# Attention with two head mixings and a feed-forward block: second batch in float32, sums in two steps, weights' conversion spread to step 90

## The chip, the cores and the metric

One core of one Trainium2 chip. The core has TensorE (PE; its weight loads are shown apart as PEld), VectorE (DVE), ScalarE (ACT), GpSimd (POOL) and SyncE (SP), which issues the DMAs; the engines run side by side, each in its own program order, and wait for each other by semaphores. The metric is the device time of one execution in microseconds; before the change it is 1026.39 us, the median of three runs (1025.78 to 1027.22).

## The reference

Four batches of 448 tokens, twelve heads of 64. The scores of all heads of a token pair are mixed by a 12 x 12 matrix before the softmax, and the attention weights by another one after it. The result, 1792 x 768, goes through a feed-forward block with 2048 hidden units. Weights come as float64.

```python
scores = scale * np.matmul(q, k.transpose(0, 1, 3, 2))
scores = np.einsum('bhij,hg->bgij', scores, w_pre)
scores = scores - np.max(scores, axis=-1, keepdims=True)
attn = np.exp(scores)
attn = attn / (np.sum(attn, axis=-1, keepdims=True) + 1e-09)
attn = np.einsum('bhij,hg->bgij', attn, w_post)
out = np.matmul(attn, v)                      # then x = out, heads side by side
h = x @ w_in
g = h * (1.0 / (1.0 + np.exp(-1.702 * h)))
return (g @ w_out).astype(np.float32)
```

## The kernel before

The work is written as a Python loop over steps, and what a step issues is the program's order on every engine; no scheduler moves it afterwards. A step i handles ten query rows of all twelve heads (120 partitions, 448 columns); 45 steps make a batch, 180 the attention. In the order of its data a group of ten rows goes through:

- scores (`scores`, lines 223 to 247): per pair of heads and chunk of 120 rows a product of q and k into two PSUM banks, copied by ScalarE and sent to a DRAM buffer `sd`, from which `gather` (line 264) reads ten rows of all heads, four steps ahead;
- `mix` (line 279): a float32 product with the 120 x 120 mixing matrix, issued one step ahead;
- `peak` (line 286), the negated row maximum on VectorE; `expo` (line 293), the exponential on ScalarE, which also sums the row; line 299, GpSimd's small epsilon-and-scale of that sum; `inverse` (line 304), VectorE's reciprocal of it;
- in batch 0 `weigh_mix` (line 309): GpSimd scales the 120 x 120 post-mixing matrix `wp` by the reciprocals, and `post_whole` (line 319) multiplies e by it in float32, four products a step, two steps behind; `keep_whole` copies the result to p;
- in batches 1 to 3 GpSimd weighs e (line 329), ScalarE writes its upper half in fp16 (line 337), GpSimd the rest (line 343), and `post` (lines 356 to 358) runs twelve fp16 products, three steps behind; ScalarE writes the upper half of p (line 379), VectorE subtracts the lower one (line 383);
- `context`: six head pairs per chunk of 120 rows, p times v: line 397 in float32 for batch 0 (8 products a pair), line 408 in fp16 halves for the others (24 products a pair), for which v is read twice, once for its size and once to be split.

Beside it run *jobs*: pieces of side work with a first step, an engine, a cost and what they come after. `run_jobs` issues in each step what is due, as long as an engine's tokens last; each step refills the tokens. `convert` makes one slice of w_in or w_out (16 in all) out of float64: three fetches, per piece five integer operations on VectorE (lines 484 to 504), a sum of squares on ScalarE, then for the slice the sum over partitions (`join_w`, by `add_all`, lines 104 to 109: a product with ones on TensorE and, right behind it in the order, VectorE's reduction of that product), its scale, an upper half on ScalarE (line 532), a lower half on VectorE (line 537) and a store to DRAM (`wd`). The slices begin at steps 5n - 6. The feed-forward work is cut into quanta of six fp16 products (lines 588 and 627), put between the attention's steps at 2.15 a step once the first batch's x is there (step 58), and dense after step 192. It fetches the converted slices from `wd` (`fetch_w`).

Of the kernel before, what the change touches and what calls it, by code (L numbers as in the profile page):

```python
# [18 lines left out]

B, H, S, D = 4, 12, 448, 64  # L20
DM, DFF = 768, 2048
NT = B * S
GI = 10
# [8 lines left out]
NS = 8  # L32
# [6 lines left out]
def attention_then_feed_forward(ctx, tc, q, k, v, w_pre, w_post, w_in, w_out, out):  # L39
# [29 lines left out]
    w_mix = keep.tile([KG, GI, H], F32, name="w_mix")  # L69
    wp = flow.tile([KG, H, GI], F32, name="wp", tag="th", bufs=2)  # L70
    wp1 = keep.tile([KG, H, GI], F16, name="wp1")
# [31 lines left out]

    def add_all(m, parts):

        p, n = parts.shape
        t = last_pp[-1][:, 512 - 16:512 - 16 + n]
        nc.tensor.matmul(t, ones[:p, :], parts, start=True, stop=True)
        nc.vector.tensor_reduce(m, t, axis=AX.X, op=ALU.add)


# [29 lines left out]

    def join(name, b):
        add_all(top_of(name, b), st["m" + name, b])

    def scale(name, b):

        m = top_of(name, b)
        e = stat.tile([128, 1], F32, name=f"e{name}_{b}", tag="e" + name)
        s = stat.tile([128, 1], F32, name=f"s_{name}{b}", tag="s" + name)
        root_bits(e, m)  # L150
        nc.vector.reciprocal(s, e)
        nc.vector.tensor_scalar_mul(s, s, 2.0 ** -50)
        nc.vector.tensor_scalar_mul(e, e, 2.0 ** 63)
        st["e" + name, b], st["s" + name, b] = e, s
        if name == "v":
            nc.vector.tensor_scalar(
                ex[:, b:b + 1], e, e_wp, 2.0 ** -12, op0=ALU.mult, op1=ALU.mult
            )
            if b == 0:
                xs = st["xs"] = keep.tile([128, 1], F32, name="xs")  # L160
                nc.vector.reciprocal(xs, ex[:, 0:1])

# [60 lines left out]
    def scores(b, c, pr, tag=("gen", 3)):  # L223

        i0, n = chunk(b, c)
        two = [bank(f"qk_{b}_{c}_{pr}_{x}", *tag) for x in range(2)]
        done = open_banks[-2:] if tag[0] == "gen" else []
        w = NPAIR // THIRDS
        if b < 2:
            qf, kf = st["q", b, pr // w], st["k", b, pr // w]  # L230
            for x in range(2):
                rs = slice(x * D, (x + 1) * D)
                nc.tensor.matmul(  # L233
                    two[x][:n, :S], qf[rs, pr % w, i0:i0 + n], kf[rs, pr % w, :],
                    start=True, stop=True,
                )
            return two, done
        qp, kp = st["qp", b, pr // w], st["kp", b, pr // w]
        terms = ((0, 0), (0, 1), (1, 0))
        for t, (i, j) in enumerate(terms):  # L240
            for x in range(2):
                rs = slice(x * D, (x + 1) * D)
                nc.tensor.matmul(  # L243
                    two[x][:n, :S], qp[rs, i, pr % w, i0:i0 + n], kp[rs, j, pr % w, :],
                    start=t == 0, stop=t == len(terms) - 1,
                )
        return two, done
# [41 lines left out]
    def expo(i):  # L289
        K = rows_of(steps[i][1])[1] * H  # L290
        e = flow.tile([KG, S], F32, name=f"e_{i}", tag="e", bufs=3)
        sm = stat.tile([KG, 1], F32, name=f"sm_{i}", tag="sm")
        nc.scalar.activation(  # L293
            e[:K], row.pop(("mx", i))[:K, :S], AF.Exp, bias=row.pop(("nm", i))[:K, 0:1],
            scale=1.0, accum_out=sm[:K, 0:1],
        )
        rs = stat.tile([KG, 1], F32, name=f"rs_{i}", tag="rs")
        by = 2.0 ** -10 if steps[i][0] else 1.0
        nc.gpsimd.tensor_scalar(rs[:K], sm[:K], 1e-9, by, op0=ALU.add, op1=ALU.mult)  # L299
        row["e", i], row["rs", i] = e, rs  # L300

# [60 lines left out]
    def mixed_to(i):  # L362
        b, g = steps[i]
        n = rows_of(g)[1]
        c, off = g // GPC, (g % GPC) * GI
        if off == 0:
            shape, kind = ([CP, NR, H, CI], F32) if b == 0 else ([CP, 2, NR, H, CI], F16)
            st["p", b, c] = mixed.tile(shape, kind, name=f"p_{b}_{c}", tag="p")
        p = st["p", b, c]
        if b == 0:  # L370
            return p.rearrange("p r h i -> p (r h) i")[:, :, off:off + n]
        return p.rearrange("p t r h i -> p t (r h) i")[:, :, :, off:off + n]
# [13 lines left out]
    def context(b, c, pr):  # L386
# [5 lines left out]
        w = H // THIRDS  # L392
        if b == 0:
            for jc in range(NR):
                for d in range(2):
                    h = 2 * pr + d
                    nc.tensor.matmul(
                        av[d * D:(d + 1) * D, pr % 3, :],
                        st["v", 0, h // w][:, h % w, jc * D:(jc + 1) * D],
                        st["p", 0, c][:, jc, h, :n],  # L400
                        start=(jc == 0), stop=(jc == NR - 1),
                    )
            return av
# [18 lines left out]
    def x_upper(b, c, half, av):  # L422
        i0, n = chunk(b, c)
        by = st["xs"] if b == 0 else 2.0 ** -15
        nc.scalar.activation(x_of(b)[:, 0, 3 * half:3 * half + 3, i0:i0 + n], av, AF.Copy, scale=by)

    def x_lower(b, c, half, av):
        i0, n = chunk(b, c)
        x = x_of(b)[:, :, 3 * half:3 * half + 3, i0:i0 + n]
        by = st["xs"] if b == 0 else 2.0 ** -15  # L430
        nc.vector.scalar_tensor_tensor(
# [3 lines left out]
    def x_size(b, c, half):  # L435
        i0, n = chunk(b, c)
        square_sum(x_of(b)[:, 0, 3 * half:3 * half + 3, i0:i0 + n],
                   st["mx", b][:, 2 * c + half:2 * c + half + 1], "A")

    def join_x(b):  # L440
        e = gs[:, b, 0:1]
        add_all(e, st["mx", b])

# [20 lines left out]
    def convert(kind, s, first):  # L464
# [45 lines left out]

        def join_w():
            t["n"] = stat.tile([128, 1], F32, name=f"{nm}_n", tag="wn")
            add_all(t["n"], t["m"])

# [31 lines left out]
        for a in range(NP):  # L546
# [11 lines left out]
            sizes.append(job(first, "A", 0.7, lambda a=a: size(a), after=[(last, 1)]))  # L558
        j = job(first, "D", 0.2, join_w, after=[(x, 1) for x in sizes])
        j = job(first, "D", 0.9, scale_w, after=[(j, 0)])  # L560
# [172 lines left out]
    for b in range(1, B):  # L733
        z = GPB * b
        sizes = {}
        if b == 1:
            for i in range(THIRDS):
                for name in "kq":
                    job(z - 23 + 4 * i, None, 0, lambda name=name, i=i: load_whole(name, 1, i), urgent=True)
        for name, first, ready in (("k", z - 25, z - 17), ("q", z - 23, z - 17), ("v", z - 8, z + LAG + 7)):  # L740
            if b == 1 and name != "v":
                continue
            sq = []
            for i in range(THIRDS):
# [3 lines left out]
                a["stage"][1].append(sq[-1])  # L748
            jn = job(0, "D", 0.2, lambda name=name, b=b: join(name, b), after=[(x, 1) for x in sq], urgent=True)
            sizes[name] = job(0, "D", 0.7, lambda name=name, b=b: scale(name, b), after=[jn], urgent=True)  # L750
            for i in range(THIRDS):
# [4 lines left out]
                a["stage"][1].extend([up, lo])  # L756
        if b > 1:
            job(0, "D", 0.4, lambda b=b: mixing(b), after=[sizes["k"], sizes["q"]], urgent=True)

    conv_done = {}  # L760
    for s in range(NS):
        for kind in range(2):
            n = s * 2 + kind
            conv_done[kind, s] = convert(kind, s, n * 5 - NPAIR if n > 1 else EARLY + 10 * n)

# [132 lines left out]
    sq = [job(1 + 2 * i, {"A": 1.6}, 0, lambda eng, i=i: squares("v", 0, i, eng, 2), urgent=True) for i in range(THIRDS)]  # L898
    j = job(1, "D", 0.2, lambda: join("v", 0), after=sq, urgent=True)
    job(1, "D", 0.9, lambda: scale("v", 0), after=[j], urgent=True)  # L900


# [49 lines left out]
    while quanta or i < N + LAG + 12:  # L952
# [8 lines left out]
        if i + 1 < N:  # L961
            mix(i + 1)
        if 0 <= i - 2 < GPB:
            post_whole(i - 2)
        if 0 <= i - 3 < GPB:
            keep_whole(i - 3)
            spend("A", 0.57)
        if GPB <= i - LAG - 1 < N:
            keep_upper(i - LAG - 1)
            spend("A", 0.55)  # L970
        if 0 <= i - 1 < GPB:
            weigh_mix(i - 1)
# [8 lines left out]
        if i < N:  # L981
            peak(i)
            spend("D", 0.62)
            expo(i)
            spend("A", 0.82)
        run_jobs(i)
# [3 lines left out]
        if owed >= 1 and do_quantum(i):  # L990
            owed -= 1
            slot()
        if GPB <= i - LAG < N:
            post(i - LAG)
# [5 lines left out]
        for b, c, pr in at_context.pop(i, []):  # L1000
# [7 lines left out]
            if c == NCH - 1 and pr == NPAIR - 1:  # L1008
                z = i
                a = job(z + 2, "D", 0.2, lambda b=b: join_x(b), urgent=True)  # L1010

                def finish(b=b, z=z):
                    scale_x(b)
                    x_done[b] = cur[0] + 1
                job(z + 3, "D", 0.9, finish, after=[a], urgent=True)
        slot()
        while owed >= 1 and do_quantum(i):
            owed -= 1
            slot()
        if GPB <= i - LAG - 1 < N:  # L1020
            keep_lower(i - LAG - 1)
            spend("D", 0.64)
        if i < N:
            inverse(i)
            spend("D", 0.15)
        owed = min(owed, 3.0)
# [44 lines left out]
```

## Time and profile before

| | |
|---|---|
| median of three runs | 1026.39 us |
| profiled execution | 1027.42 us, span 1025.7 us |
| PE / DVE / ACT / POOL busy | 925.0 / 628.8 / 605.2 / 354.5 us |
| mean granted TensorE clock | 0.961 |
| DMA | 198.19 MB, mean 193 GB/s |
| chain that ended last | PE 62%, DVE 17%, ACT 8%, DMA 8%, issue 3% |

Busy times are unions within an engine; products on TensorE overlap, so the time from one start to the next tells what a product costs, not its own length. The steps can be told by the row maxima of line 286, one a step: step 0 starts at 34.8 us, step 45 at 196.6, step 58 at 257.9, step 90 at 444.2, step 103 at 497.8, step 179 at 864.1.

### The profile page before, as it was taken

The numbers are of one execution on the slowest core, as the hardware profiler recorded it, in microseconds if no ns is written. First come the engines' busy times: TensorE is split into PE (matmuls) and PEld (weight loads), VectorE is DVE, ScalarE is ACT, GpSimd is POOL, SyncE is SP. The second block draws the span as 40 slices with busy tenths as digits, with TensorE's granted clock in tenths as the row PEclk, the third lists the DMA queues.
The fourth block names the chain that finished last, engine by engine and source line by source line (L and its number), as shares of the span: only waits on it lengthen the run. The fifth ranks groups of instructions, "written<-read, shape, count | busy, mean of one in ns | idle before, by whom it ended". The sixth has DMA issues, their size and how long they took to land.

```text
span 1025.7 us, 19868 instructions
## 1 busy us (share of the span) xinstructions
PE 925.0 (90%) x7344; PEld 542.4 (53%) x7344; DVE 628.8 (61%) x1389; ACT 605.2 (59%) x1380; POOL 354.5 (35%) x536
## 2 busy tenths in 40 slices
PE   5678878877899889999899999999899999999998
PEld 4345555544455444555455555656455666555554
DVE  5658786698976796554644575555645565443334
ACT  3666768677577676765657657656656564323332
POOL 0111111145433455343533454334534444001221
PEclk9888999888999998999999999999999999999999
DMA  8988979768557656654676647546654341234322
GB/s 301 289 275 313 332 267 323 259 197 245 190 198 244 232 187 181 192 172 131 202 225 207 202 150 234 166 130 179 212 164 146 108 148 64 93 123 151 118 93 85
DMA packets 66565, 198.19 MB, mean 193 GB/s; under 512 B 7668, under 2 KB 32372, under 8 KB 66468
## 3 DMA queue, kind: packets, MB, share of 16 engines
q1 hardware_dynamic: 66064, 196.83, 59.4%
q8 instruction: 58, 0.95, 0.4%
q14 instruction: 39, 0.32, 0.1%
q10 hardware_dynamic: 404, 0.09, 0.1%
HBM read 140.27 MB, written 56.62 MB: 192 GB/s over the span
## 4 chain that ended last, share of the span: by engine, by line
PE 62%; DVE 17%; ACT 8%; DMA 8%; issue 3%; POOL 1%; SPq 0%; ACTq 0%; DVEq 0%; POOLq 0%
PE po L627 19%; PE h L588 18%; PE mx L279 8%; PE av L408 4%; PE qk L243 3%; PE pp L356 2%; PE pp L358 2%; PE pp L357 2%; DVE w_p L537 2%; DMA sd<-sc 2%; ACT waste L96 2%; DVE w_f L504 2%; DMA w<-in_moe_w_out_dram 2%; DVE nm L286 2%; ACT e L293 1%
## 5 line engine op out<-in xcount | busy, mean ns | idle before, releaser
L627 PE MATMUL po<-g,wt 128*128 128x448 f16 x1152 | 243.8, 355 | 11.3 <-DVE th L609 6.8
L588 PE MATMUL h<-x,wt 128*128 128x448 f16 x1152 | 244.1, 356 | 3.9 <-ACT sc L253 2.9
L279 PE MATMUL mx<-r,wa 120*120 120x448 f32 x360 | 183.3, 592 | 40.0 <-ACT e L293 29.7
L343 POOL TENSOR_TENSOR a<-w,a 120x448 f16<-120x448 f32 x135 | 150.8, 1117 | 130.2 <-issue 71.5
L627 PEld LDWEIGHTS <-wt 128*128 128x128 f16 x1152 | 109.4, 99 | 130.0 <-issue 45.1
L588 PEld LDWEIGHTS <-wt 128*128 128x128 f16 x1152 | 109.2, 98 | 117.0 <-issue 31.2
L329 POOL TENSOR_SCALAR w<-e,rs 120x448 f32<-120x448 f32 x135 | 88.2, 653 | 227.3 <-DVE rs L304 217.8
L337 ACT ACTIVATE a<-e,rs 120x448 f16<-120x448 f32 x135 | 91.0, 674 | 106.1 <-DVE rs L304 106.1
L657 DVE SCALAR_TENSOR_TENSOR acc<-po,ct,acc 128x448 f32<-128x448 f32 x141 | 96.1, 682 | 74.3 <-PE po L627 72.2
L293 ACT ACTIVATE e<-mx,nm 120x448 f32<-120x448 f32 x180 | 113.6, 631 | 31.2 <-POOL wr L309 25.4
L609 DVE SCALAR_TENSOR_TENSOR th<-th,h 128x448 f32<-128x448 f32 x64 | 39.7, 620 | 137.8 <-ACT th L606 137.8
L606 ACT ACTIVATE th<-h,ct 128x448 f32<-128x448 f32 x64 | 40.5, 633 | 140.2 <-PE h L588 129.6
L253 ACT COPY sc<-qk 120x448 f32<-120x448 f32 (+1 forms) x186 | 89.6, 532 | 41.8 <-PE qk L233 28.9
L286 DVE TENSOR_REDUCE nm<-mx 120x1 f32<-120x448 f32 x180 | 108.9, 605 | 1.9 <-PE mx L279 1.9
L356 PE MATMUL pp<-wp,a 120*112 120x120 f16 x540 | 95.7, 220 | 14.8 <-DVE p L383 14.3
L279 PEld LDWEIGHTS mx<-r,wa 120*120 120x120 f32 x360 | 61.6, 193 | 83.9 <-ACT e L293 47.0
L299 POOL TENSOR_SCALAR rs<-sm 120x1 f32<-120x1 f32 x180 | 56.8, 315 | 115.8 <-ACT e L293 103.8
L358 PE MATMUL pp<-wp,a 120*112 120x120 f16 x540 | 95.1, 219 | 0.0
L357 PE MATMUL pp<-wp,a 120*112 120x120 f16 x540 | 94.9, 218 | 0.0
L383 DVE TENSOR_TENSOR p<-pp,p 112x480 f16<-112x480 f32 x135 | 87.2, 647 | 5.9 <-ACT p L379 5.9
L356 PEld LDWEIGHTS <-a 120*112 120x112 f16 x540 | 71.5, 132 | 26.9 <-DVE p L383 12.1
L357 PEld LDWEIGHTS <-a 120*112 120x112 f16 x540 | 71.8, 133 | 15.9 <-issue 9.5
(126 smaller groups left out, 1258.1 us busy)
## 6 DMA issues: line engine op xcount, KB each, us to landing
wt<-wd SPq DMA_DIRECT2D x64, 768.0 KB
r<-sd SPq DMA_DIRECT2D x176, 210.0 KB
sd<-sc SPq DMA_DIRECT2D x72, 420.0 KB
w<-in_moe_w_in_dram SPq DMA_DIRECT2D x24, 512.0 KB
w<-in_moe_w_out_dram SPq DMA_DIRECT2D x24, 512.0 KB
wd<-w_p SPq DMA_DIRECT2D x16, 768.0 KB
sd<-sc SPq DMA_DIRECT2D x24, 308.0 KB
out_dram<-acc SPq DMA_DIRECT2D x24, 224.0 KB
```

The lines of the kernel that those rows point to most:

```text
L253: (nc.scalar.copy if engs[x] == "A" else nc.vector.tensor_copy)(t[:n, x, :], two[x][:n, :S])
L279: nc.tensor.matmul(mx[:K, :S], st["wa", b][:K, :K], row.pop(("r", i))[:K, :], start=True, stop=True)
L286: nc.vector.tensor_reduce(nm[:K], row["mx", i][:K, :S], axis=AX.X, op=ALU.max, negate=True)
L293: nc.scalar.activation(e[:K], row.pop(("mx", i))[:K, :S], AF.Exp, bias=row.pop(("nm", i))[:K, 0:1], scale=1.0, accum_out=sm[:K, 0:1],)
L337: nc.scalar.activation(a1[:K], row.pop(("e", i))[:K], AF.Copy, scale=row.pop(("rs", i))[:K, 0:1])
L343: nc.gpsimd.tensor_tensor(a2[:K], row.pop(("w", i))[:K], row["a1", i][:K], op=ALU.subtract)
L356: nc.tensor.matmul(o, a1[:K, js], wp1[:K, :, :n], start=True, stop=False)
L357: nc.tensor.matmul(o, a1[:K, js], wp2[:K, :, :n], start=False, stop=False)
L358: nc.tensor.matmul(o, a2[:K, js], wp1[:K, :, :n], start=False, stop=True)
L588: nc.tensor.matmul(h, w[:, i, c, fc * 128:(fc + 1) * 128], x[:, j, c, :], start=(n == 0), stop=(n == len(terms) - 1),)
L627: nc.tensor.matmul(po, w[:, j, fc, e * 128:(e + 1) * 128], g[:, i, fc, :], start=(n == 0), stop=(n == len(terms) - 1),)
L657: nc.vector.scalar_tensor_tensor(a, po, c, a, op0=ALU.mult, op1=ALU.add)
```

## The change

A constant WHOLE = 2 takes the place of the tests for batch 0: batch 1 goes through `weigh_mix`, `post_whole`, `keep_whole` and the float32 context as well, and its v is read once, at steps 52, 54 and 56. `wp` gets a place of its own, as it now lives to step 91. `add_all` falls into two jobs (`sum_jobs`): the product with ones in one step, VectorE's reduction in the next. `expo` loses its small GpSimd operation, which becomes `shifted` and is issued after the weighing of the step before; the reciprocal of step i - 1 is issued in step i, behind the row maximum; the weighing of step i - 1 comes behind the exponential of step i. The conversions begin at steps 7n - 12 up to n = 8, then 5.5 steps apart, the last at step 82 and stored at step 96 (before: 69 and 83). The quanta of the feed-forward stand in the same steps as before.

```diff
-    def add_all(m, parts):
+    def add_over(parts):
         p, n = parts.shape
         t = last_pp[-1][:, 512 - 16:512 - 16 + n]
         nc.tensor.matmul(t, ones[:p, :], parts, start=True, stop=True)
+        return t
+
+    def add_along(m, t):
         nc.vector.tensor_reduce(m, t, axis=AX.X, op=ALU.add)
+
+    def sum_jobs(first, m, parts, after):
+        t = {}
+        def over():
+            t["t"] = add_over(parts())
+        j = job(first, None, 0, over, after=after, urgent=True)
+        return job(first, "D", 0.2, lambda: add_along(m(), t["t"]), after=[j], urgent=True)
...
+    def shifted(i):
+        K = rows_of(steps[i][1])[1] * H
+        sm = row.pop(("sm", i))
         rs = stat.tile([KG, 1], F32, name=f"rs_{i}", tag="rs")
-        by = 2.0 ** -10 if steps[i][0] else 1.0
+        by = 1.0 if steps[i][0] < WHOLE else 2.0 ** -10
         nc.gpsimd.tensor_scalar(rs[:K], sm[:K], 1e-9, by, op0=ALU.add, op1=ALU.mult)
...
-        if b == 1:
+        if b < WHOLE:
...
+                a = job(z + 7 + 2 * i, None, 0, lambda i=i, b=b: load_whole("v", b, i), urgent=True)
...
-            conv_done[kind, s] = convert(kind, s, n * 5 - NPAIR if n > 1 else EARLY + 10 * n)
+            begin = EARLY + 10 * n if n < 2 else 7 * n - 12 if n <= NS else 11 * (n - NS) // 2 + 7 * NS - 12
+            conv_done[kind, s] = convert(kind, s, begin)
...
-        if 0 <= i - 2 < GPB:
+        if 0 <= i - 2 < WHOLE * GPB:
             post_whole(i - 2)
...
+        if i < N:
+            peak(i)
+            spend("D", 0.62)
+        if 0 <= i - 1 < N:
+            inverse(i - 1)
+            spend("D", 0.15)
+        if i < N:
+            expo(i)
+            spend("A", 0.82)
-        if 0 <= i - 1 < GPB:
+        if 0 <= i - 1 < WHOLE * GPB:
             weigh_mix(i - 1)
             spend("G", 0.35)
         elif 0 <= i - 1 < N:
...
             lower(i - 1)
             spend("G", 1.07)
         if i < N:
-            peak(i)
-            spend("D", 0.62)
-            expo(i)
-            spend("A", 0.82)
+            shifted(i)
         run_jobs(i)
...
-        if i < N:
-            inverse(i)
-            spend("D", 0.15)
```

TensorE at a post-mixing of batch 1, before the change, behind a quantum (h is the hidden product, pp the result, a the two fp16 halves of the weighed e):

```order
L588 LDWEIGHTS wt_2_2859
L588 MATMUL h_0_3381<-x_995,wt_2_2859 128x448
L356 LDWEIGHTS a_63_3214
L356 MATMUL pp_3429<-wp_84,a_63_3214 112x120
L357 LDWEIGHTS a_63_3214
L357 MATMUL pp_3429<-wp_85,a_63_3214 112x120
L358 LDWEIGHTS a_63_3216
L358 MATMUL pp_3429<-wp_84,a_63_3216 112x120
```
And with the change, at the same rows of the matrix (wr is the weighed mixing matrix, e the exponential):

```order
L290 MATMUL mx_2901<-r_2698,wa_255 120x448
L335 MATMUL pp_2903<-wr_2853,e_2776 112x120 x4
L639 LDWEIGHTS wt_0_564
L639 MATMUL po_5_2927<-g_2508,wt_0_564 128x448
L639 LDWEIGHTS wt_0_564
```
Twelve fp16 products with their weight loads became four float32 products, and they stand right behind the next step's mixing instead of behind a quantum.

VectorE at a slice's sum in batch 0, before (nm is the row maximum, w_2_n the sum, rs the reciprocal):

```order
L286 TENSOR_REDUCE nm_1055<-mx_1003 120x1
L109 TENSOR_REDUCE w_2_n<-pp_1047 128x1
L81 TENSOR_SCALAR w_2_n<-w_2_n 128x1
L82 TENSOR_SCALAR ew<-w_2_n 128x1
L518 TENSOR_SCALAR ew<-ew 128x1
L520 RECIPROCAL w_2_s<-ew 128x1
L521 TENSOR_SCALAR w_2_s<-w_2_s 128x1
L304 RECIPROCAL rs_1060<-rs_1060 120x1
L286 TENSOR_REDUCE nm_1099<-mx_1045 120x1
```
And with the change:

```order
L297 TENSOR_REDUCE nm_1145<-mx_1102 120x1
L320 RECIPROCAL rs_1118<-rs_1118 120x1
L113 TENSOR_REDUCE w_2_n<-pp_1104 128x1
L82 TENSOR_SCALAR w_2_n<-w_2_n 128x1
L83 TENSOR_SCALAR ew<-w_2_n 128x1
L530 TENSOR_SCALAR ew<-ew 128x1
L532 RECIPROCAL w_2_s<-ew 128x1
L533 TENSOR_SCALAR w_2_s<-w_2_s 128x1
L297 TENSOR_REDUCE nm_1181<-mx_1137 120x1
```
The reduction of the sums stood in the step of TensorE's product with ones and now stands a step later; the reciprocal, which closed a step, now follows the next maximum.

SyncE's queue at the store of the last slice of w_in (wd_7_113) before, in step 78, with the row gathers (r) and score stores (sd) behind it; the slice's fetch stands 21 rows further, in step 86:

```order
L543 DMA wd_7_113<-w_7_p 128x3072
L269 DMA r_4458<-sd_3_97 120x448
L269 DMA r_4527<-sd_3_97 120x448
L258 DMA sd_0_98<-sc_0_0_4515 120x896
L269 DMA r_4596<-sd_3_97 120x448
L576 DMA wt_6_4598<-wd_6_112 128x3072
```
And with the change, in steps 90 and 91:

```order
L555 DMA wd_7_113<-w_7_p 128x3072
L269 DMA sd_1_99<-sc_1_2_4451 120x896
L280 DMA r_4529<-sd_0_98 120x448
L588 DMA wt_7_4531<-wd_7_113 128x3072
L280 DMA r_4582<-sd_0_98 120x448
L588 DMA wt_8_4584<-wd_0_106 128x3072
```
Store and fetch of this slice (wt_7_4531<-wd_7_113) now stand three rows apart, with one gather between them and the next behind; its first product is in step 93 in both programs.

## Rows read from the trace of the kernel before

**Rows 1.** Busy us of PE, PEld, DVE, ACT, POOL; clock, DMA share, GB/s

```profile
34.70:196.50 161.80, 130.09 (x803) 81.74 (x802) 119.15 (x309) 117.35 (x299) 30.15 (x90) 0.92 0.88 299
196.50:257.80 61.30, 46.23 (x343) 28.10 (x342) 49.92 (x110) 40.89 (x95) 26.78 (x38) 0.84 0.69 213
257.80:444.10 186.30, 166.83 (x1377) 94.91 (x1377) 135.55 (x281) 129.00 (x294) 80.19 (x103) 0.95 0.63 205
444.10:497.70 53.60, 50.99 (x506) 30.90 (x505) 30.05 (x70) 34.35 (x79) 25.56 (x39) 1.00 0.58 167
```

**Rows 2.** The same stretches, row maxima (line 286) alone, one a step

```profile
34.70:196.50 161.80, 27.25 (x45) 0.92 0.88 299
196.50:257.80 61.30, 7.87 (x13) 0.84 0.69 213
257.80:444.10 186.30, 19.34 (x32) 0.95 0.63 205
497.70:864.00 366.30, 45.96 (x76) 1.00 0.54 168
```

**Rows 3.** The same view, VectorE's instructions on pieces of weights (tile w_f)

```profile
34.70:196.50 161.80, 80.19 (x147) 0.92 0.88 299
196.50:257.80 61.30, 32.34 (x46) 0.84 0.69 213
257.80:444.10 186.30, 46.58 (x65) 0.95 0.63 205
```

**Rows 4.** Waits in 34.7 to 257.8: who, for whom; us, times, longest

```profile
PE mx L279 <- ACT e L293: 26.6, 18, 5.2
DVE w_n L109 <- PE pp L108: 21.6, 11, 5.2
DVE rs L304 <- POOL rs L299: 20.2, 18, 3.3
```

**Rows 5.** DMA issues of the page: count, KB each

```profile
w<-in_moe_w_in_dram SPq DMA_DIRECT2D x24, 512.0 KB
wd<-w_p SPq DMA_DIRECT2D x16, 768.0 KB
```

**Rows 6.** Timeline of TensorE in batch 0: start us, us, instruction

```profile
154.06 0.98 PE L319 MATMUL pp<-wr,e 120*112 120x120 f32 x8
154.98 1.04 PE L397 MATMUL av<-p,vf 112*64 112x120 f32 x16
155.95 1.01 PE L279 MATMUL mx<-r,wa 120*120 120x448 f32 x2
```

**Rows 7.** Timeline of TensorE, one fp16 post-mixing (batch 2): its first product, and the next work

```profile
510.93 0.22 PE L356 MATMUL pp<-wp,a 120*112 120x120 f16 x1
...
511.56 1.30 PE L588 MATMUL h<-x,wt 128*128 128x448 f16 x6
```

**Rows 8.** Timeline of TensorE in batch 2, feed-forward work between

```profile
641.08 0.78 PE L243 MATMUL qk<-kp,qp 64*120 64x448 f16 x6
641.79 0.82 PE L408 MATMUL av<-p,vp 112*64 112x120 f16 x24
642.54 1.01 PE L279 MATMUL mx<-r,wa 120*120 120x448 f32 x2
643.39 1.30 PE L627 MATMUL po<-g,wt 128*128 128x448 f16 x6
644.53 0.22 PE L356 MATMUL pp<-wp,a 120*112 120x120 f16 x1
```

**Rows 9.** Waits in 257.8 to 444.1

```profile
PE pp L356 <- DVE p L383: 10.1, 6, 3.3
```

**Rows 10.** Groups by line and shape: count, busy us, mean ns; idle before

```profile
L383 DVE TENSOR_TENSOR p<-pp,p 112x480 f16<-112x480 f32 x132 | 85.6, 649 | 5.9 <-ACT p L379 5.9
...
L309 POOL TENSOR_SCALAR wr<-wp,rs 120x120 f32<-120x120 f32 x44 | 16.1, 366 | 65.9 <-DVE rs L304 60.3 <-PE pp L319 3.1 <-PE mx L279 1.8
```

**Rows 11.** Pieces of the chain that ended last: start us, us, what

```profile
49.80 9.79 DMA wd<-w_p
```

More of the change, by code (lines that the diff above doesn't have):

```diff
@@ L20 @@
 B, H, S, D = 4, 12, 448, 64
+WHOLE = 2
 DM, DFF = 768, 2048
@@ L69, in attention_then_feed_forward @@
     w_mix = keep.tile([KG, GI, H], F32, name="w_mix")
-    wp = flow.tile([KG, H, GI], F32, name="wp", tag="th", bufs=2)
+    wp = keep.tile([KG, H, GI], F32, name="wp")
     wp1 = keep.tile([KG, H, GI], F16, name="wp1")
@@ L140, in top_of @@
         return tops[:, i:i + 1]
-    def join(name, b):
-        add_all(top_of(name, b), st["m" + name, b])
     def scale(name, b):
@@ L158, in scale @@
             )
-            if b == 0:
-                xs = st["xs"] = keep.tile([128, 1], F32, name="xs")
-                nc.vector.reciprocal(xs, ex[:, 0:1])
+            if b < WHOLE:
+                xs = st["xs", b] = keep.tile([128, 1], F32, name=f"xs_{b}")
+                nc.vector.reciprocal(xs, ex[:, b:b + 1])
     def mixing(b):
@@ L228, in scores @@
         w = NPAIR // THIRDS
-        if b < 2:
+        if b < WHOLE:
             qf, kf = st["q", b, pr // w], st["k", b, pr // w]
@@ L296, in expo @@
         )
+        row["e", i], row["sm", i] = e, sm
+    def shifted(i):
+        K = rows_of(steps[i][1])[1] * H
+        sm = row.pop(("sm", i))
         rs = stat.tile([KG, 1], F32, name=f"rs_{i}", tag="rs")
-        by = 2.0 ** -10 if steps[i][0] else 1.0
+        by = 1.0 if steps[i][0] < WHOLE else 2.0 ** -10
         nc.gpsimd.tensor_scalar(rs[:K], sm[:K], 1e-9, by, op0=ALU.add, op1=ALU.mult)
-        row["e", i], row["rs", i] = e, rs
+        row["rs", i] = rs
     def inverse(i):
@@ L366, in mixed_to @@
         if off == 0:
-            shape, kind = ([CP, NR, H, CI], F32) if b == 0 else ([CP, 2, NR, H, CI], F16)
+            shape, kind = ([CP, NR, H, CI], F32) if b < WHOLE else ([CP, 2, NR, H, CI], F16)
             st["p", b, c] = mixed.tile(shape, kind, name=f"p_{b}_{c}", tag="p")
         p = st["p", b, c]
-        if b == 0:
+        if b < WHOLE:
             return p.rearrange("p r h i -> p (r h) i")[:, :, off:off + n]
@@ L392, in context @@
         w = H // THIRDS
-        if b == 0:
+        if b < WHOLE:
             for jc in range(NR):
@@ L398, in context @@
                         av[d * D:(d + 1) * D, pr % 3, :],
-                        st["v", 0, h // w][:, h % w, jc * D:(jc + 1) * D],
-                        st["p", 0, c][:, jc, h, :n],
+                        st["v", b, h // w][:, h % w, jc * D:(jc + 1) * D],
+                        st["p", b, c][:, jc, h, :n],
                         start=(jc == 0), stop=(jc == NR - 1),
@@ L423, in x_upper @@
         i0, n = chunk(b, c)
-        by = st["xs"] if b == 0 else 2.0 ** -15
+        by = st["xs", b] if b < WHOLE else 2.0 ** -15
         nc.scalar.activation(x_of(b)[:, 0, 3 * half:3 * half + 3, i0:i0 + n], av, AF.Copy, scale=by)
@@ L429, in x_lower @@
         x = x_of(b)[:, :, 3 * half:3 * half + 3, i0:i0 + n]
-        by = st["xs"] if b == 0 else 2.0 ** -15
+        by = st["xs", b] if b < WHOLE else 2.0 ** -15
         nc.vector.scalar_tensor_tensor(
@@ L438, in x_size @@
                    st["mx", b][:, 2 * c + half:2 * c + half + 1], "A")
-    def join_x(b):
-        e = gs[:, b, 0:1]
-        add_all(e, st["mx", b])
     def scale_x(b):
@@ L509, in size, with total @@
             square_sum(t["f", a].bitcast(F32), t["m"][:, a:a + 1], "A")
-        def join_w():
+        def total():
             t["n"] = stat.tile([128, 1], F32, name=f"{nm}_n", tag="wn")
-            add_all(t["n"], t["m"])
+            return t["n"]
         def scale_w():
@@ L558, in convert @@
             sizes.append(job(first, "A", 0.7, lambda a=a: size(a), after=[(last, 1)]))
-        j = job(first, "D", 0.2, join_w, after=[(x, 1) for x in sizes])
+        j = sum_jobs(first, total, lambda: t["m"], [(x, 1) for x in sizes])
         j = job(first, "D", 0.9, scale_w, after=[(j, 0)])
@@ L735, in attention_then_feed_forward @@
         sizes = {}
-        if b == 1:
+        if b < WHOLE:
+            sq = []
             for i in range(THIRDS):
                 for name in "kq":
-                    job(z - 23 + 4 * i, None, 0, lambda name=name, i=i: load_whole(name, 1, i), urgent=True)
+                    job(z - 23 + 4 * i, None, 0, lambda name=name, i=i, b=b: load_whole(name, b, i), urgent=True)
+                a = job(z + 7 + 2 * i, None, 0, lambda i=i, b=b: load_whole("v", b, i), urgent=True)
+                sq.append(job(0, {"A": 1.6}, 0, lambda eng, i=i, b=b: squares("v", b, i, eng, 2), after=[(a, SENT)], urgent=True))
+            j = sum_jobs(0, lambda b=b: top_of("v", b), lambda b=b: st["mv", b], sq)
+            job(0, "D", 0.9, lambda b=b: scale("v", b), after=[(j, 0)], urgent=True)
+            continue
         for name, first, ready in (("k", z - 25, z - 17), ("q", z - 23, z - 17), ("v", z - 8, z + LAG + 7)):
-            if b == 1 and name != "v":
-                continue
             sq = []
@@ L748, in attention_then_feed_forward @@
                 a["stage"][1].append(sq[-1])
-            jn = job(0, "D", 0.2, lambda name=name, b=b: join(name, b), after=[(x, 1) for x in sq], urgent=True)
-            sizes[name] = job(0, "D", 0.7, lambda name=name, b=b: scale(name, b), after=[jn], urgent=True)
+            jn = sum_jobs(0, lambda name=name, b=b: top_of(name, b), lambda name=name, b=b: st["m" + name, b], sq)
+            sizes[name] = job(0, "D", 0.7, lambda name=name, b=b: scale(name, b), after=[(jn, 0)], urgent=True)
             for i in range(THIRDS):
@@ L756, in attention_then_feed_forward @@
                 a["stage"][1].extend([up, lo])
-        if b > 1:
-            job(0, "D", 0.4, lambda b=b: mixing(b), after=[sizes["k"], sizes["q"]], urgent=True)
+        job(0, "D", 0.4, lambda b=b: mixing(b), after=[sizes["k"], sizes["q"]], urgent=True)
     conv_done = {}
@@ L898, in attention_then_feed_forward @@
     sq = [job(1 + 2 * i, {"A": 1.6}, 0, lambda eng, i=i: squares("v", 0, i, eng, 2), urgent=True) for i in range(THIRDS)]
-    j = job(1, "D", 0.2, lambda: join("v", 0), after=sq, urgent=True)
-    job(1, "D", 0.9, lambda: scale("v", 0), after=[j], urgent=True)
+    j = sum_jobs(1, lambda: top_of("v", 0), lambda: st["mv", 0], sq)
+    job(1, "D", 0.9, lambda: scale("v", 0), after=[(j, 0)], urgent=True)
     at_scores = {}
@@ L962, in attention_then_feed_forward @@
             mix(i + 1)
-        if 0 <= i - 2 < GPB:
+        if 0 <= i - 2 < WHOLE * GPB:
             post_whole(i - 2)
-        if 0 <= i - 3 < GPB:
+        if 0 <= i - 3 < WHOLE * GPB:
             keep_whole(i - 3)
             spend("A", 0.57)
-        if GPB <= i - LAG - 1 < N:
+        if WHOLE * GPB <= i - LAG - 1 < N:
             keep_upper(i - LAG - 1)
             spend("A", 0.55)
-        if 0 <= i - 1 < GPB:
+        if i < N:
[8 more added lines that the diff above has]
+        if 0 <= i - 1 < WHOLE * GPB:
             weigh_mix(i - 1)
@@ L992, in attention_then_feed_forward @@
             slot()
-        if GPB <= i - LAG < N:
+        if WHOLE * GPB <= i - LAG < N:
             post(i - LAG)
@@ L1009, in attention_then_feed_forward @@
                 z = i
-                a = job(z + 2, "D", 0.2, lambda b=b: join_x(b), urgent=True)
+                a = sum_jobs(z + 2, lambda b=b: gs[:, b, 0:1], lambda b=b: st["mx", b], [])
                 def finish(b=b, z=z):
@@ L1014, in finish @@
                     x_done[b] = cur[0] + 1
-                job(z + 3, "D", 0.9, finish, after=[a], urgent=True)
+                job(z + 3, "D", 0.9, finish, after=[(a, 0)], urgent=True)
         slot()
@@ L1019, in attention_then_feed_forward @@
             slot()
-        if GPB <= i - LAG - 1 < N:
+        if WHOLE * GPB <= i - LAG - 1 < N:
             keep_lower(i - LAG - 1)
             spend("D", 0.64)
-        if i < N:
-            inverse(i)
-            spend("D", 0.15)
         owed = min(owed, 3.0)
```

## The prediction

> **What bounds the kernel now.** I read first the busy time by stage, cut at starts of the row-maximum on VectorE, one per step, then the waits, the chain, and the timelines of TensorE. The stages hold 45, 13 and 32 steps, then 13 and 76 [rows 1, 2]. The reader is to see three kinds of stage. In the first (34.7 to 196.5 us, batch 0, 3.60 us a step) the DMA engines are 88% busy at 299 GB/s and no compute engine is over 81%: transfers come first, and behind them the chain score mixing, maximum, exponential, in which TensorE waited 26.6 us in sum for the exponential [rows 4]. In the second and third (196.5 to 444.1, 4.72 and 5.82 us a step) VectorE is busy 81% and 73% while the DMA share falls to 0.69 and 0.63. In the fourth TensorE is busy 95% and sets the pace.
>
> What TensorE needs for a step with feed-forward work, read start to start [rows 7, 8]: mixing 643.39 - 642.54 = 0.85; post-mixing 511.56 - 510.93 = 0.63; a context pair 0.75 and a score pair 641.79 - 641.08 = 0.71, 24 of each per 45 steps, so 0.40 and 0.38; a quantum of six products 644.53 - 643.39 = 1.14, at the code's rate of 2.15 a step 2.45. Together 4.71 us. The last stage of steps took 366.3 / 76 = 4.82, which is that need and 2%. Steps 58 to 89 took 5.82: about 1.11 x 32 = 36 us in which TensorE was kept waiting, some of it behind the subtraction that fills the lower half of p (10.1 us) [rows 9].
>
> **The change part by part.** (1) *Batch 1 in float32, on TensorE.* A float32 post-mixing runs 154.98 - 154.06 = 0.92 us, a float32 context pair 155.95 - 154.98 = 0.97 [rows 6], against 0.63 and 0.75: 45 x 0.29 + 24 x 0.22 = 18.3 us more TensorE time, of which 11 posts (3.2 us) fall into the second stage, 32 posts and 18 pairs (13.2) into the third, the rest (1.9) into the fourth. (2) *Batch 1, off TensorE.* On VectorE 45 subtractions of 0.649 us go (29 us) [rows 10], and three splits of v; on ScalarE the fp16 copy of e and on GpSimd two passes of 448 columns become one of 120. (3) *Conversions.* By the two formulas the fetches that begin in steps 0 to 44 are nine before (4, 9, ... 44) and seven after (2, 9, ... 44), the stores there eight and seven. One conversion is three fetches of 512 KB and one store of 768 KB [rows 5], and 18 VectorE instructions on its pieces: 80.19 / 147 x 18 = 9.8 us in the first stage, 12.9 in the third, where GpSimd is busier [rows 3]. The first stage loses two, the second keeps about 2.5, the third rises from 3.6 to about 5, the fourth gets nearly one that it did not have. (4) *Sums in two steps and the later reciprocal.* VectorE stood 21.6 us for the sums' product and 20.2 us for the reciprocal's input before 257.8 us [rows 4]; both should go, since a step now lies between. The reciprocal comes behind the next maximum, 0.6 us later, and the weighing behind the next exponential; post-mixing, a step after the weighing, has the slack. Were that cover gone, the weighing's 0.366 us [rows 10] would lie on the path in 45 steps of batch 1: 16 us, which I cost at nothing and keep for the wide end.
>
> By stage. **Steps 0 to 44.** Bytes leave: 2 x 1.57 + 0.79 MB of weights, and 1.38 MB of v that batch 1 read here a first time (three pieces of 112 x 1024 float32): 5.3 MB, 17.7 us at 299 GB/s. If transfers set all of it the gain is 17.7, if latencies do it is near 0; a loss is excluded, since no engine and no queue gets more to do there. The row nearest is the DMA share of 0.88, so I take most of it: -13, which is 3.31 us a step, still above TensorE's 130.1 / 45 = 2.89 busy. **Steps 45 to 57.** 61.3 us. VectorE's 49.9 loses 10 x 0.649; its waits go as well. TensorE's busy 46.2 + 3.2 = 49.4 is the floor: between 0 and -12, taken near the floor because VectorE was the fullest engine: -11. **Steps 58 to 89.** TensorE's need becomes 4.71 + 0.29 + 0.22 x 18 / 32 = 5.12 a step, 164 us: the best is 186.3 - 164 = -22. If the 36 us of waiting stay, it is +13. VectorE's 135.6 loses 32 x 0.649 = 20.8 for p and gains 1.4 conversions (14); five conversions also become cheaper by up to 3.1 us each, with GpSimd emptier: 114 to 129, so 3.6 to 4.0 us a step against TensorE's 5.12, where it was 4.24 against 4.71. I take 175 us, midway between floor and today: -11. **Steps 90 to 102.** The late conversions end here: +1.9 us of TensorE, and one new wait. The last slice of w_in is stored at step 90, fetched back at 91 and used at 93; before, eight steps lay between store and fetch. The fetch waits on SyncE for the store, with the row gathers behind it, which are four steps ahead and thereby covered. A store stood for 9.79 us in the chain once, early, on busy DMA [rows 11]; two steps are 9.4 us, and DMA is at 0.58 here. From 0 to 10 us; I take 1 for this: +3. **From step 103.** Only the order of maximum, reciprocal, exponential and weighing differs: -6 to +4, taken -2, since TensorE waits hardly ever.
>
> Sum: -13 - 11 - 11 + 3 - 2 = -34. The profiled execution took 1027.42 us (span 1025.7), so 993.4; the median of the runs shown is 1.0 lower: 992.4, I say 992.
>
> **A rule against the first term.** The first stage moves 299 GB/s with the DMA engines at 0.88 [rows 1]. The Trainium skill (HBM Reference, Specifications (TRN2)) has a core that streams alone well above its share, at about 425 GB/s. By that the memory is not full at 299, and the stage would be held by latency and small packets; no run here shows 425. It is the first rival.
>
> **Rivals.** *Latency, not bytes, holds steps 0 to 57.* For it: the DMA share is not 1, and the chain jumps between engines. Against it: 0.88 as a mean over sixteen engines for 160 us. Then the first term is 0 and the second half, -5: 1027.4 - 5 - 11 + 3 - 2 = 1012, less 1.0: 1011. *The floors are reached.* For it: the waits of VectorE that go (41.8 us) and the spread of its bursts remove just what TensorE waits for. Then -18 - 14 - 20 + 1 - 4 = -55: 971. *TensorE pays in full.* One mechanism, on the other side: from step 45 the 18.3 us of float32 are added to the path while the waits of TensorE stay, because the conversions that now reach into steps 83 to 95 refill VectorE with bursts of five instructions on a piece, ahead of the maximum. It decides if the third stage does not fall below 186 us. Price: +18.3 and 3, and the first term then at -13 is used up: 1027.4 + 21.3 - 13 - 1 = 1035. For it: TensorE is already 90% busy in that stage. Against: the busy share there counts overlapping drains, and the step's need is 4.71 of 5.82. *It does nothing:* the reciprocal's input comes no earlier than before and the savings cancel the price: 1026.
>
> **How the numbers follow.** Forecast 0.52, latency 0.15, floors 0.20, full price 0.10, nothing 0.03. A difference of 0.2% (2 us) is about what a measurement of this kernel can tell from none. Faster 0.52 + 0.15 + 0.20 = 0.87, same 0.03, slower 0.10. The range holds the forecast with the ends of its terms and reaches both neighbours: 966 to 1020; the full price lies outside.
>
> **What would show it.** Right: first stage near 149 us at about the same DMA share and fewer bytes; second near 50; third near 175 with TensorE's post-mixing at four instructions and VectorE without its subtraction; hardly any VectorE wait for the sums' product or the reciprocal's input. A wait of TensorE for the w_in slice at step 93 would show the fourth term. Wrong: a first stage that keeps 3.6 us a step while its DMA share falls (latency), or a third stage at 186 us or more with VectorE's bursts ahead of the maximum.

## The result and the profile after

The changed kernel takes 991.1 us (median of four runs, 990.11 to 991.31) against 1026.8 us; the ratio is 0.9641, 95% interval 0.9609 to 0.9673. The forecast was 992. The profiled execution took 991.19 us, its span 989.3 us, so 36.4 us less span than before.

The stages of the changed kernel, cut at the same row maxima (columns: from:to, us, then busy time and instructions of PE, PEld, DVE, ACT and POOL, granted clock, DMA share, GB/s):

```profile
35.70:176.30 140.60, 122.95 (x805) 77.79 (x804) 100.63 (x259) 105.02 (x267) 33.26 (x89) 0.99 0.86 292
176.30:225.40 49.10, 42.93 (x320) 28.50 (x319) 34.76 (x91) 34.41 (x89) 10.46 (x26) 0.97 0.85 284
225.40:399.00 173.60, 165.26 (x1088) 98.04 (x1088) 123.93 (x292) 118.74 (x282) 47.88 (x76) 0.98 0.72 235
399.00:456.60 57.60, 55.22 (x452) 32.97 (x449) 29.36 (x74) 39.18 (x91) 29.52 (x41) 1.00 0.64 189
456.60:826.10 369.50, 355.30 (x3177) 210.24 (x3175) 214.14 (x442) 223.40 (x506) 162.84 (x233) 0.99 0.54 167
```

Beside [rows 1] and the last row of [rows 2]: the first stage falls by 21.2 us, the second by 12.2, the third by 12.7, the fourth rises by 4.0, the fifth by 3.2; the start takes 1.0 more and the dense end 1.5. In the first stage TensorE's busy time falls by 7.1 us and its idle time by the rest, 14; the granted clock rises from 0.92 to 0.99. That the DMA share stays (0.88, 0.86) while 292 x 140.6 = 41.1 MB move instead of 48.4 (7.3 fewer, where the forecast had 5.3) looks like a stage held by transfers. The experiments say otherwise.

VectorE's instructions on pieces of weights in the first and the third stage of the changed kernel (busy us, count, clock, DMA):

```profile
35.70:176.30 140.60, 61.33 (x111) 0.99 0.86 292
225.40:399.00 173.60, 61.08 (x102) 0.98 0.72 235
```

Against [rows 3] the first stage has two conversions less (36 instructions, 18 for each), the third two more, and one costs 61.08 / 102 x 18 = 10.8 us there, where it cost 12.9.

Waits of the changed kernel in its first stage (who, for whom; us, times, longest):

```profile
PE mx L290 <- ACT e L304: 12.9, 14, 1.7
DVE rs L320 <- POOL rs L315: 10.5, 16, 2.2
DVE w_n L113 <- ACT p L391: 7.3, 5, 2.3
```

[rows 4] reach over the second stage as well. In the first stage alone (34.7 to 196.5 us) the kernel before had, for the first of these:

```profile
PE mx L279 <- ACT e L293: 19.9, 15, 5.2
```

and 17.1 us for the second, the reciprocal's input. VectorE no longer waits for the sums' product itself, which took 15.1 us there; its reduction still waits 7.3 us, put down to ScalarE's copy of p. So the waits of VectorE became shorter and did not vanish.

### The profile page after: what moved, and what is told of

It reads as the page before. It is cut to its first block, busy times and chain, and to the rows that moved or that the text cites. A ratio compares the mean times of both kernels' runs of the same rounds, so it can differ in the third digit from the quotient of the medians.

```text
span 989.3 us, 18926 instructions
## 1 busy us (share of the span) xinstructions
PE 921.2 (93%) x6972; PEld 544.9 (55%) x6972; DVE 588.6 (59%) x1333; ACT 581.7 (59%) x1342; POOL 313.8 (32%) x500
## 4 chain that ended last, share of the span: by engine, by line
PE 67%; DVE 16%; ACT 8%; DMA 5%; issue 3%; POOL 0%; ACTq 0%; SPq 0%; DVEq 0%
PE h L600 19%; PE po L639 19%; PE mx L290 9%; PE pp L335 4%; PE av L424 3%; PE av L413 3%; PE qk L244 2%; PE qk L254 2%; DVE nm L297 2%; DVE w_f L510 2%; ACT e L304 2%; PE pp L372 2%; PE pp L374 2%; PE pp L373 2%; DVE w_f L516 2%
## 5 line engine op out<-in xcount | busy, mean ns | idle before, releaser
L359 POOL TENSOR_TENSOR a<-w,a 120x448 f16<-120x448 f32 (+1 forms) x90 | 95.9, 1065 | 102.8 <-issue 46.7
L335 PEld LDWEIGHTS pp<-wr,e 120*112 120x112 f32 x720 | 89.0, 180 | 36.5 <-issue 30.4
L325 POOL TENSOR_SCALAR wr<-wp,rs 120x120 f32<-120x120 f32 (+1 forms) x90 | 54.8, 609 | 166.7 <-DVE rs L320 119.8
L345 POOL TENSOR_SCALAR w<-e,rs 120x448 f32<-120x448 f32 (+1 forms) x90 | 66.0, 733 | 124.5 <-DVE rs L320 70.5
L315 POOL TENSOR_SCALAR rs<-sm 120x1 f32<-120x1 f32 x180 | 46.7, 260 | 142.0 <-ACT e L304 132.3
L335 PE MATMUL pp<-wr,e 120*112 120x120 f32 x720 | 90.3, 269 | 0.0
L666 POOL TENSOR_TENSOR acc<-acc,pt 128x448 f32<-128x448 f32 x37 | 43.6, 1179 | 129.6 <-ACT pt L663 128.7
L372 PE MATMUL pp<-wp,a 120*112 120x120 f16 x360 | 62.4, 217 | 3.8 <-DVE p L399 1.9
L320 DVE RECIPROCAL rs<-rs 120x1 f32<-120x1 f32 x180 | 28.1, 156 | 61.8 <-POOL rs L315 61.6
L628 DVE SCALAR_TENSOR_TENSOR g<-th,gs,g 128x448 f16<-128x448 f32 x64 | 50.3, 785 | 20.8 <-ACT g L625 19.8
```

The lines of the kernel that those rows point to most:

```text
L325: nc.gpsimd.tensor_scalar(t[:K], wp[:K], row.pop(("rs", i))[:K, 0:1], 1.0, op0=ALU.mult, op1=ALU.mult)
L335: nc.tensor.matmul(pp[:CP, jc * K:(jc + 1) * K], e[:K, jc * CP:(jc + 1) * CP], wr[:K, :, :n], start=True, stop=True,)
L345: nc.gpsimd.tensor_scalar(w[:K], e[:K], row["rs", i][:K, 0:1], 1.0, op0=ALU.mult, op1=ALU.mult)
L359: nc.gpsimd.tensor_tensor(a2[:K], row.pop(("w", i))[:K], row["a1", i][:K], op=ALU.subtract)
L372: nc.tensor.matmul(o, a1[:K, js], wp1[:K, :, :n], start=True, stop=False)
```

## Experiments

Seven kernels put on or take off one part; the two loads ask what holds the first stage; the rest ask about price and order. Times are medians; ratios are against the kernel before on the same chip, with 95% intervals. Its medians there are 1028.2 us beside the four parts put on alone, 1029.5 beside the three taken off and the added bytes, and 1027.7 beside the others. Stages are read from one profiled execution of each kernel; where the program of the first stage is that of the changed kernel (two profiles of it, and two kernels that differ only later), that stage took 139.4 to 140.6 us.

**The later starts alone.** `+ begin = ... 7 * n - 12 if n <= NS else ...` on the kernel before.

> Only the later starts of the conversions, on the kernel before. If bytes set steps 0 to 44 (my theory), that stage falls from 161.8 to about 147 us alone by this (3.9 MB of weights less at 299 GB/s = 13), steps 58 to 89 rise by 5 to 10 because batch 1 still subtracts on VectorE: about 1018 in all. If the stage was held by VectorE's waits for sums and reciprocal (rival), it stays above 156 us and the whole is 1026 or more.

1036.0 us, ratio 1.0056 (1.0032 to 1.0080): slower by less than 1%, where 1018 was expected. Its first and third stage:

```profile
34.80:195.10 160.30, 132.64 (x804) 82.93 (x804) 100.18 (x267) 111.03 (x283) 26.97 (x90) 0.92 0.82 274
251.10:451.20 200.10, 171.95 (x1379) 97.63 (x1379) 161.35 (x321) 135.15 (x310) 84.19 (x106) 0.93 0.65 209
```

The first stage moved 274 x 160.3 = 43.9 MB, 4.5 less than before, at a lower rate, in the same time. The forecast's first term, as bytes, falls here. VectorE had 19 us less work and stood instead: these are its waits in that stage.

```profile
DVE rs L314 <- POOL rs L309: 27.4, 23, 3.9
DVE w_n L113 <- PE pp L109: 11.8, 7, 2.9
DVE w_f L490 <- DMA w<-in_moe_w_out_dram: 7.7, 3, 4.2
```

The third stage shows the other half: with batch 1 still subtracting, the added conversions bring VectorE to 161 of 200 us, and the stage grows by 13.8.

**Batch 1 in float32 alone.** `+ WHOLE = 2` with all its tests, nothing else.

> Only batch 1 in float32, on the kernel before. My theory: steps 0 to 44 lose 1.4 MB of v, 4 us; steps 45 to 57 lose 7, steps 58 to 89 lose 8, nothing is paid later: about 1007. Rival (TensorE pays its 18.3 us in full): 1040.

1011.6 us, ratio 0.9814 (0.9784 to 0.9845). The second stage took 53.5 us (-7.8), the third 175.3 (-11.0), the first 159.6 (-2.2), from the fourth on nothing was paid beyond 1.3 us. The rival that TensorE pays in full is refuted. VectorE in the third stage falls from 135.6 to 102.6 us.

**Sums in two steps alone.** `+ j = job(first, None, 0, over, ...)`, VectorE's reduction as a second job.

> Only the sums over partitions in two steps, on the kernel before. My theory: VectorE's 21.6 us of waiting before 257.8 us go, but transfers hold that stage: 1 to 4 us, 1023 in all. Rival (VectorE's waits hold steps 0 to 57): 10 us or more, below 1017.

1031.9 us, ratio 1.0027 (0.9998 to 1.0057): no change that can be told. The first stage did fall, by 8.0 us to 153.8, though not by the shorter wait alone: 132 instructions on pieces of weights stand in it, where there were 147. The third took 198.1 us, with VectorE busy 149.6 where it was 135.6 and 81 of these instructions where there were 65: conversions had moved later, into the stage where VectorE was already the fullest beside TensorE.

**The later reciprocal alone.** `+ inverse(i - 1)` behind `peak(i)`, weighing behind the exponential.

> Only the later reciprocal and weighing, on the kernel before. My theory: 0 to -4 us before step 58, 0 to +4 from step 103 on, where the changed kernel is 3.2 us slower than before: 1026. Rival (VectorE's 20.2 us of waiting for the reciprocal's input held the early stages): below 1016.

1037.6 us, ratio 1.0065 (1.0040 to 1.0089), first stage 162.0. VectorE's wait for the reciprocal's input was mostly gone there (6.5 us, from 17.1) and the stage did not care; its wait for the sums' product had grown from 15.1 to 19.0. What this kernel lost, it lost in the second stage (+2.0), from step 103 on (+5.4) and at the end (+1.2).

Alone, the four parts take 1.5, 2.2, 8.0 and -0.2 us from the first stage, 11.5 in sum; together 21.2. So I took three of them off, one at a time; the fourth, batch 1 in float32, was not taken off the full change.

**All but the spread; all but the two-step sums; all but the later reciprocal.** Each is the changed kernel with one part as before.

> The changed kernel with the conversions back at their earlier starts. The spread alone did nothing for steps 0 to 44 (160.4 us), so bytes did not hold them. New theory: in that stage VectorE's in-order waits for sums, reciprocal and fetched weights each delay a row maximum, TensorE stops and runs at half clock; all have to go together. Then this kernel keeps sums and reciprocal but has dense bursts: steps 0 to 44 at 148 to 154 us, the whole at 1000. If the four parts simply added, it would be 991 less the 8 that the spread cost alone: 983.

> The changed kernel with the sum's product and its reduction in one step again. Alone the two-step sums took 8 us from steps 0 to 44 and lost 12 in steps 58 to 89. New theory (waits that go together): the first stage back to 148 to 154 us with VectorE waiting some 15 us for the product, the whole at 999. If the parts added: 991 less 3 to 5, since the sums alone made the kernel no faster.

> The changed kernel with the reciprocal and the weighing in their old places. Alone the later reciprocal cost 9 us, of which 5 from step 103 on and 2 in the second stage. If the parts add: 982, with steps 103 to 178 back at 366.3 us. If the waits have to go together (new theory): the first stage is at 147 or more, as VectorE waits some 25 us for the reciprocal's input, and the late stage gains 3 to 5: 991 to 996.

994.4 us (0.9671, 0.9644 to 0.9699), 998.7 (0.9709, 0.9680 to 0.9738) and 991.6 (0.9640, 0.9609 to 0.9671). The first stage is 146.4, 148.7 and 141.4 us, where the whole change has 140.6. The new theory fits the sums, and roughly the spread. Neither theory fits the reciprocal, whose absence costs nothing that can be told: 991.6 lies in the new theory's range, but the first stage is not at 147 or more, though VectorE waits there as long as expected:

```profile
DVE rs L320 <- POOL rs L315: 26.5, 18, 2.9
```

The spread, worth 1.5 us alone, is worth 5.8 here. The sums are worth 8.1, and here VectorE's busy time is the same with and without them (100.5 and 100.6 us), so that the wait is what differs. Waits of the kernel with one-step sums in that stage:

```profile
DVE w_n L113 <- PE pp L109: 17.5, 7, 4.7
PE mx L284 <- ACT e L298: 15.0, 16, 4.2
```

The granted clock there was 0.96 without two-step sums and 0.95 without the spread (0.99 and 0.98 in two profiles of the whole change). One of the longer waits of the kernel with one-step sums (TensorE's timeline: start, us, instruction, idle before it):

```profile
79.12 1.01 PE L284 MATMUL mx<-r,wa 120*120 120x448 f32 x2 [4.15 <-ACT e L298]
79.97 1.61 PE L329 MATMUL pp<-wr,e 120*112 120x120 f32 x8
```

From 80 to 84 us the clock there is 0.57, that is mostly 1.2 instead of 2.4 GHz, and the post-mixing takes 1.61 us, not the 0.98 of [rows 6]. Such stretches are part of why TensorE's own work takes 126.3 and 125.3 us in these two kernels, against 123.0.

**More bytes; more VectorE work.** On the changed kernel, in steps 1 to 39:

```diff
...
+        nc.sync.dma_start(out=st["more"][:, n % 2], in_=w_in[n % NS][:, :512].bitcast(I32))
...
+    for n in range(10):
+        job(1 + 4 * n, None, 0, lambda n=n: more(n), urgent=True)
```

```diff
...
+        for _ in range(3):
+            nc.vector.tensor_scalar_max(junk, junk, TINY)
+        for _ in range(2):
+            nc.vector.scalar_tensor_tensor(junk, junk, 1.0, junk, op0=ALU.mult, op1=ALU.mult)
...
+    for n in range(7):
+        job(3 + 6 * n, None, 0, lambda n=n: burst(n), urgent=True)
```

> The changed kernel with ten more loads of 512 KB of weights in steps 1 to 37, into a place that nobody reads: 5.2 MB, about what the change took from the first stage. If bytes set that stage (the forecast's first term), it grows by 17 us to 158 and the whole to 1008. If latencies of VectorE's queue do (new theory), by 0 to 5: 991 to 996.

> The changed kernel with 35 more VectorE instructions of 128 x 512 in steps 3 to 39, seven bursts of five on a place that nobody reads, about 19 us. If VectorE's queue ahead of the row maximum holds steps 0 to 44, that stage of 140.6 us grows by 8 us or more, with more half-clock time. If transfers hold it, by less than 3: the ten more loads cost 6.9.

999.0 us (0.9723, 0.9686 to 0.9759) and 1004.2 (0.9776, 0.9747 to 0.9804). First stages, bytes and then VectorE:

```profile
35.60:183.10 147.50, 127.85 (x797) 80.00 (x798) 100.96 (x259) 105.38 (x267) 32.54 (x89) 0.94 0.91 314
36.20:185.70 149.50, 123.87 (x802) 78.74 (x803) 118.14 (x293) 105.25 (x267) 32.40 (x90) 0.97 0.82 276
```

5.2 MB cost 6.9 us, more than the new theory's 0 to 5 and less than the 17.5 that 299 GB/s would make; 17.5 us of VectorE cost 8.9. Neither holds the stage alone, and in these profiles each is paid for by some 40 to 50% of itself. The bytes are paid mostly in TensorE's own work (4.9 us more busy, 2.0 more idle, at a clock of 0.94), VectorE's work mostly in waiting (0.9 more busy, 8.0 more idle). The 8.9 is not exact: that profile is the kernel's fastest execution, 998.25 us, and by medians the load costs 10.9 us against the changed kernel on the same chip; and 2.4 us of VectorE's waiting in it are for GpSimd, which fills the place before the first burst. The queue took the added bytes at 314 GB/s, so 299 was no ceiling. The Trainium skill (HBM Reference, Specifications (TRN2)) has about 425 GB/s for a core that streams alone. The trace agrees in that 314 lies above 299; no run here shows 425.

**The third batch in float32 as well.** `WHOLE = 3` for its post-mixing, context and v; its scores stay fp16.

> The changed kernel with the third batch's post-mixing and context in float32 too; its scores stay fp16. There TensorE sets the pace, so the price stands uncovered: 18.3 us by the forecast's rows less the few us of TensorE's waits that VectorE's lost subtractions and splits remove (gaps of 14 us from step 103 to 178): 1003 to 1009. If VectorE's relief were what batch 1 gained by wherever it stands, 991 or less.

995.7 us (0.9693, 0.9659 to 0.9728), against 993.3 for the changed kernel on the same chip: the intervals overlap, and the full price I expected, 1003 to 1009, is not there. Steps 103 to 178 of it:

```profile
459.80:832.80 373.00, 366.19 (x2839) 219.56 (x2839) 185.15 (x410) 206.29 (x476) 114.62 (x198) 0.99 0.53 163
```

TensorE's busy time is 10.9 us up, the stage 3.5; in steps 90 to 102 they are up 1.7 and 3.2. The price itself is smaller than I read. A float32 post-mixing inside feed-forward work of this kernel, and an fp16 one of the changed kernel with a context product behind it (TensorE's timeline: start, us, instruction):

```profile
508.61 0.98 PE L335 MATMUL pp<-wr,e 120*112 120x120 f32 x8
509.43 1.30 PE L639 MATMUL po<-g,wt 128*128 128x448 f16 x6
```

```profile
421.66 0.22 PE L372 MATMUL pp<-wp,a 120*112 120x120 f16 x1
...
422.38 0.83 PE L413 MATMUL av<-p,vf 112*64 112x88 f32 x16
```

With feed-forward products behind it, float32 costs 0.82 us and fp16 0.63 [rows 7]; with a context product behind it 0.92 [rows 6] and 0.72. So with the same kind of work behind both, the difference is 0.19 or 0.20 us, not 0.29: I had set the 0.92 before a context product against the 0.63 before a hidden one. By this the third batch costs TensorE 45 x 0.19 + 24 x 0.22 = 13.8 us; its busy time rose by 12.6 in the two stages, and they took 6.7 longer.

**The old order from step 90 on, and the changed kernel again.** `early = i <= WHOLE * GPB`: later reciprocal and weighing for batches 0 and 1 alone.

> The changed kernel with the later reciprocal in batches 0 and 1 alone and the old order from step 90 on. In the changed kernel steps 103 to 178 took 369.5 us and the rest 163.1, against 366.3 and 161.6 before; the kernel with the old order everywhere got 3.8 us of this back and lost 2 to 3 before step 90. If the two effects are apart, this one takes both: 987. If the early stages drift by as much from run to run, it stays at 991.

> The changed kernel once more, on the same chip as the one with the split order: 990 to 992 us if it repeats, to be set against the 987 expected of that one.

987.7 us (0.9614, 0.9587 to 0.9641) and 993.3 (0.9662, 0.9635 to 0.9688). The split order has the lower median, by 5.6 us, with intervals that just overlap, so that it beats the changed kernel is likely and not settled. The profiled executions do not help: they are the slowest of this kernel (990.1 us) and the fastest of the other (990.9). Nor does this one show the reason I gave: the late stage is at 369.6 us as in the changed kernel, clock 0.99; only the dense end gave back its 1.4 us. And the kernel with more VectorE work, whose order there is that of the changed kernel, ran that stage in 367.0 us at a clock of 1.00. Steps 103 to 178 of every profiled execution with fp16 there, in us, by granted clock:

| clock | old order there | new order there |
|---|---|---|
| 1.00 | 366.3 (before; spread alone), 366.4 (float32 alone), 367.1 (no later reciprocal) | 367.0 (more VectorE work) |
| 0.99 | 368.3 (sums alone), 369.6 (split order) | 368.7 (no spread), 369.4 (more bytes), 369.5 (changed kernel, twice) |
| 0.98 | | 370.8 (no two-step sums), 371.7 (reciprocal alone) |

The stage goes with its clock: at the same clock the two orders lie in one range. With the new order the clock was below 1.00 in six of seven, with the old one in two of six, so that the order may still be what lowers it; the runs do not settle that.

## Why the prediction was right

The sum was -34 and the span fell by 36.4; three of five terms were near, and the largest had the wrong cause. That the sum came so close is in part luck: the first stage gave 8.2 us more than forecast, and everything from step 103 on took 6.7 more.

- **Steps 0 to 44, forecast -13 by bytes, measured -21.2.** This step failed in its mechanism. Taking 4.5 MB away alone gained 1.5 us, giving 5.2 MB back cost 6.9, and 299 GB/s was exceeded. So bytes are worth 1.5 to 6.9 us by these two tests. What the runs show in its place is waits in VectorE's order, ahead of the row maximum: the wait for the sums' product, worth 8.1 us when it is put back, and the dense conversions, worth 5.8 (with 2.4 MB more in the stage), though spreading them alone gained 1.5. Of the 21.2 us, 7.1 are TensorE's own work at a higher clock and 14 its waiting. The nearest of the forecast's rivals, latency, had the cause right but priced it at 0. The later reciprocal, of which I expected that its 20.2 us go, did nothing. That removing one wait lets the next one bind is what these numbers suggest, not something that a run isolates; the share of batch 1 in float32, and which pairs of parts suffice, were not run.
- **Steps 45 to 57, -11, measured -12.2; steps 58 to 89, -11, measured -12.7.** Right, and mostly by the cause given: batch 1 off VectorE alone makes -7.8 and -11.0. The two floors were set wrong. The second stage's, 46.2 + 3.2 = 49.4 us, was added up from TensorE's busy time at a clock of 0.84; at 0.97 that engine was busy 42.9 us and the stage took 49.1, under that floor. That the forecast came near here is in part luck. The third stage's, 164 us, was too high by 32 x 0.10 = 3, as the float32 price was.
- **Price of float32, 18.3 us.** Mis-sized: the post-mixing costs 0.19 us more instead of 0.29, so 8.6 us instead of 13; with the context's 5.3 some 14. I had read 0.92 where a context product followed, and 0.63 where a hidden one did.
- **Steps 90 to 102, +3, measured +4.0,** but not by the wait named: TensorE waited for a fetched slice 0.2 us in the whole execution. The store was issued at 396.21 us and the fetch behind it at 401.88, 14 us before step 93; none of SyncE's waits from 395 to 425 us is put down to the store:

```profile
396.21 0.38 SPq L555 DMA_DIRECT2D wd<-w_p  x1
...
401.88 0.40 SPq L588 DMA_DIRECT2D wt<-wd  x1
```

With the spread taken off, the fourth stage is 54.4 us and the third 176.3, in sum 230.7 against 231.2. So most of the 4 us is work of TensorE that an earlier row maximum moved across the cut: at step 90's maximum TensorE had begun 184 mixing and 423 feed-forward products before the change, 182 and 414 after it. Third and fourth stage together are -8.7, forecast -8.
- **From step 103, -2, measured +3.2 and 1.5 at the end.** Wrong in sign. The end follows the order: 161.6 to 161.8 us in the six profiled executions with the old order there, 162.9 to 163.2 in the eight with the new one. The stage follows its clock, as the table above shows; that the order lowers the clock is not shown.

## What to carry to other kernels

In a stage where an engine waits in order for several others, the length of a wait does not tell what it is worth: with the change in place, 26.5 us of VectorE's waiting for the reciprocal cost 0.8 us, and 17.5 us of waiting for the sums cost 8.1. Measure parts by taking them off the full change as well as by putting them on. Work moved to a later stage pays only if that stage has had room made for it: spreading the conversions cost 8 us alone, and beside the relief of VectorE it gained 3, with intervals that overlap. Read a product's price where the same kind of work follows it, in both of its forms.

## What was not expected

- TensorE's idle time carries a second price in its clock: in the first stage 0.92 and 130.1 us busy before, 0.99 and 123.0 us after, for the same post-mixing, mixing and score products. It is not the sum of idle time that counts: with more VectorE work TensorE stood 25.6 us in that stage at 0.97, with more bytes 19.7 us at 0.94.
- A rate of 299 GB/s at a DMA share of 0.88 over 160 us was no sign of a limit: the same queue took 314 GB/s at 0.91, and 4.5 MB less alone gained 1.5 us of 161.8.
- The fp16 split of an operand into two halves, three products for one, saves TensorE only 0.19 us of 0.82 on 120 columns. It costs VectorE a subtraction of 0.65 us [rows 10], and ScalarE and GpSimd a pass more each.
